# mLSTM and Fourier mixing on one core: recurrent outputs of batches 2 to 4 with tokens on partitions, and rows shifted by DMA

## The chip, the cores and the metric

The kernel runs on one core of a Trainium2 chip. The metric is the device time of one execution in microseconds (us). The time before is the median of three runs, 405.04 us (404.22, 408.13 and 405.04).

Five engines run their own instruction streams, each in order, and wait for each other by semaphores: TensorE (PE; its weight loads are shown apart as PEld), VectorE (DVE), ScalarE (ACT), GpSimd (POOL) and SyncE (SP). SP issues the DMAs of the kernel before. SBUF and PSUM have 128 partitions; a tile is written "partitions x elements".

## What is computed

Four batches, 8 heads, 768 tokens, 40 features per head, all float32. First a recurrence over tokens, per batch and head:

```python
for t in range(S):
    m_new  = np.maximum(f_gate[t] + m, i_gate[t])
    f_stab = np.exp(f_gate[t] + m - m_new); i_stab = np.exp(i_gate[t] - m_new)
    C = f_stab * C + i_stab * outer(v[t], k[t])      # 40 x 40
    n = f_stab * n + i_stab * k[t]                   # 40
    y[t] = sigmoid(o_gate[t]) * (C @ q[t]) / max(abs(n @ q[t]), 1)
```

Its output, with heads side by side, is x of 768 x 320 per batch. Then:

```python
u  = x + real(fft(fft(x, axis=seq), axis=feature))
un = (u - mean(u)) / sqrt(var(u) + 1e-6)
out = u + relu(un @ w1) @ w2                         # 320 -> 1280 -> 320
```

## The kernel before

**Order of the work.** A hand-written plan puts every piece of work at a place with `at(slot, phase, function, ...)`; pieces are sorted by slot and phase and issued in that order, which fixes the order on each engine. Within a slot the phases are EVAC, FILL, MAIN and FILL_PE. From slot 31 on, each batch's MLP owns the MAIN phase of 32 slots (batch 1: 31 to 62, batch 2: 63 to 94, batch 3: 95 to 126, batch 4: 127 to 158). What a later batch needs is filled in around it. For batches 2 to 4 (index b = 1 to 3) the first 20 slots are `mlp_block` (L1074), in rounds of four steps, in which TensorE writes bank after bank (pm), ScalarE copies the first product of a bank out and VectorE adds the others to the hidden layer (L1093); the next 12 slots are `mlp_out_pair` (L1191). Batch 1 uses an older form of both.

**The recurrence.** It runs in six chunks of 128 tokens. For batch 1 `plan_mlstm` plans it, with 128-token tiles. For batches 2 to 4 `plan_halves` does, with each chunk in two halves of 64 tokens, so that four products of 64 x 64 tiles run beside each other on TensorE (`product`, L491, tiles chosen by TILES). Chunk c starts at slot s = s0 + 3c; s0 is 32, 50 and 82 for batches 2, 3 and 4. In it:

- `halves_scores` and `halves_to_state` (TensorE): scores k by q into ps, and what the chunk adds to the state C; `halves_decay` (POOL, L629) and `halves_add` (VectorE, L638) update C;
- W is the table of decay weights: a DMA brings row maxima (M_d), ScalarE takes exponentials (L464), POOL masks it to causal (`mlstm_mask`, L487), VectorE multiplies it with the scores (`halves_weigh`, L643). `mlstm_scale_q` (POOL, L474) multiplies q with decays that a DMA brings from G_d;
- `halves_from_state` and `halves_from_chunk` (slot s+3): the output, numerator and the 41st column n @ q, into the head bank ph. Here the weights are C (or v) and the moving operand the queries (or W), 64 columns wide, so the output has features on partitions and tokens along the row. `halves_between` (L670) is a one-element ScalarE copy, warm, which separates the two halves of `halves_from_chunk`;
- `halves_gather` (ScalarE, L568 to L579) copies ph to SBUF as hT; `halves_turn` (TensorE, L681) transposes it in four pieces back into ph, tokens on partitions; `mlstm_finish` (VectorE, L696 to L703) makes the denominator and writes x, multiplied with the gate so.

The turns are at s0 + (7, 10, 13, 16, 19, 19) and the finishes one slot later. The last chunk has from-state and from-chunk in the MAIN phase, around an MLP matmul.

**Backward chunks.** The Fourier transform over tokens is folded: chunk pairs (0,5), (1,4) and (2,3) are added and subtracted (`mix_fold`, VectorE, L778 to L790). For this, chunks 2, 4 and 5 (BACKWARDS) are stored with their tokens reversed and shifted by one row. Before, that is done in `halves_gather`, which copies tokens reversed, with the odd token out handled by two small copies and by POOL (h_first). The folds of batches 3 and 4 are at s0 + 18 for the pair (2,3), s0 + 21 for (1,4) and s0 + 23 for (0,5). When x is folded, its tables are multiplied with the transform matrices (pz, pu), and its statistics follow.

**Set up on the way.** `halves_of_chunks` (L307 and on) makes the tables for batches 2 to 4 beside batch 1's recurrence: g to G_d (step 1), and with TensorE transposes and a spreading matmul colT and decB (steps 3 and 4). `maxima_out` writes M_d. colT holds per-token columns that ScalarE's exponentials and POOL's scaling of v (L480) use.

Of the kernel before, what the change touches and what calls it, by code (L numbers as in the profile page):

```python
# [10 lines left out]
FP = mybir.dt.float32  # L11
# [31 lines left out]
ORDER = (0, 5, 1, 4, 2, 3)  # L43
M_INIT = -1.0e30
# [8 lines left out]
def kernel(  # L53
# [87 lines left out]
    def gates(gp):  # L141
# [161 lines left out]

        def maxima_out():
            nc.sync.dma_start(out=M_d.rearrange("c i p t -> p c i t"), in_=M[0:BH].rearrange("p c (i t) -> p c i t", i=2))

        def halves_of_chunks(step):  # L307
# [8 lines left out]
            elif step == 1:  # L316
# [3 lines left out]
                nc.sync.dma_start(out=G_d[:, H:].rearrange("c p t -> p c t"), in_=g[H:BH])  # L320
# [12 lines left out]
            else:  # L333
                pt, pd = late["p2"]
                nc.vector.tensor_copy(out=colT[:, :, 1, H:], in_=pt[:, :, H:])  # L335
                nc.vector.tensor_copy(out=decB[:, NP:], in_=pd[:, NP:])

        at(12, FILL + 0.7, maxima_out)
        at(1, FILL + 0.2, parts, last)
# [9 lines left out]
        for n, (s, phase) in enumerate(((16, FILL + 0.2), (18, FILL + 0.3), (19, FILL + 0.4), (21, FILL_PE + 0.5),  # L349
                                        (26, FILL + 0.8))):  # L350
            at(s, phase, halves_of_chunks, n)
# [132 lines left out]
    def mlstm_mask(b, c):  # L484
        for i in range(2):
            W = chunks[b, c].W[i * LH:(i + 1) * LH]
            nc.gpsimd.affine_select(out=W, in_=W, compare_op=OP.is_ge, fill=0.0, base=0, pattern=[[0, H], [1, LH]],  # L487
                                    channel_multiplier=-1)
# [70 lines left out]
    def mlstm_heads(b, c, ph, parts=False):  # L559
# [3 lines left out]
        if b > 0:  # L563
            hT, before = (t.rearrange("p (hip m) t -> p hip m t", hip=2) for t in (hT, before))
        every, first, later = (tuple([slice(None)] * (len(ph.shape) - 1) + [t]) for t in
                               (slice(0, L), slice(0, 1), slice(1, L)))
# [27 lines left out]
    def side(n):  # L594
        return banks["heads"].rearrange("p hip (s m t) -> p s hip m t", s=2, t=L)[:, n]

    TILES = ((0, 0), (1, 1), (0, 1), (1, 0))

    def columns(c, n):

        return LH if c == 0 else n

    def halves_scores(b, c):
# [5 lines left out]
        for p in range(NP):  # L609
            for hip, i in TILES:  # L610
                r, t = slice(hip * 64, hip * 64 + D), slice(i * LH, (i + 1) * LH)
                product(k.ps[t, hip, p, :], k.qk[r, 1, p, t], k.qk[r, 0, p, t], True)

    def halves_to_state(b, c):
        k = chunks[b, c]
        for p in range(NP):
            for i, hip in TILES:
                if 2 * c + i < NS - 1:
                    r, h, n = slice(i * LH, (i + 1) * LH), hip * NP + p, columns(c, D)
                    product(k.pc[hip * 64:hip * 64 + n, i, p, :], k.k[r, h * D:h * D + n], k.vw[r, h, :], True)  # L620
# [11 lines left out]
    def halves_add(b, c, i):  # L632

        k, n = chunks[b, c], 2 * c + i
        if n == 0:
            nc.vector.tensor_copy(out=halves_state(k, 1), in_=k.pc[:, 0])
        elif n < NS - 1:
            nc.vector.tensor_tensor(out=halves_state(k, i + 1), in0=halves_state(k, i + 1), in1=k.pc[:, i], op=OP.add)  # L638
# [6 lines left out]
    def halves_from_state(b, c):  # L645

        k = chunks[b, c]
        k.ph = side(0)
        for m in range(2):
            for i in range(2):  # L650
                for hip, e in TILES:
                    if 2 * c + i > 0:
                        r, t, p = slice(hip * 64, hip * 64 + D), slice(i * LH, (i + 1) * LH), 2 * m + e
                        product(k.ph[e * 64:(e + 1) * 64, hip, m, t], k.C[i][r, p * D1:p * D1 + LH], k.qg[r, p, t],
                                m == 0 and i == (c == 0))

    def halves_from_chunk(b, c, turn):
# [4 lines left out]
        for m in range(2):  # L662
            for i, e in TILES:
                hip, n = i ^ turn, columns(c, D1)
                r, h = slice(i * LH, (i + 1) * LH), hip * NP + 2 * m + e
# [780 lines left out]
```

## Time and profile before

The profile is of one execution of 410.02 us, with a span of 408.3 us from first to last instruction, at a mean granted clock of 0.991 of full speed. That execution is 4.98 us over the median of the three timed runs.

| engine | busy us | share of span | instructions |
|---|---|---|---|
| TensorE matmul | 390.9 | 96% | 4246 |
| TensorE weight load | 285.3 | 70% | 4246 |
| VectorE | 281.3 | 69% | 669 |
| ScalarE | 182.1 | 45% | 510 |
| GpSimd | 129.1 | 32% | 228 |

| what the change touches | lines | time |
|---|---|---|
| transposes of the heads, 72 | PE L681 | 10.5 us, 275 ns each |
| ScalarE copies of the heads | L568, L575 | 583 and 588 ns each |
| finish, last product, 18 | DVE L703 | 8.8 us, 491 ns each |
| weighing of the scores, 18 | DVE L643 | 12.3 us, 682 ns each |
| DMA queue of all transfers | q1 | 35.8% of 16 engines' span |

How to read it: "busy" counts overlapping instructions of one engine once in the share and singly in a group's sum, so a group of matmuls that overlap has a sum that is longer than the time it takes. A row of a group names line, engine and operation, then output <- inputs, shapes and count, and after the bar busy time, mean time of one, and how long the engine had stood idle just before, with what ended it. In the list of waits, each row names an instruction, what it waited for, and the sum, the number and the longest of the waits. A slice line gives the busy share of 40 equal slices in tenths. "Issue" as a releaser means that the profile shows nothing the engine waited for.

### The profile page before, as it was taken

The page shows a single profiled execution, that of the slowest core. Times are in us where ns is not written, and L with a number is a line of the kernel's source. Part 1 is how long each engine was busy: PE and PEld are TensorE (multiplying, and loading weights), DVE is VectorE, ACT ScalarE, POOL GpSimd, SP SyncE. Part 2 cuts the span into 40 slices and gives each one's busy share as a digit, 9 for nine tenths or more (in the row PEclk, how much of TensorE's full clock was granted, in tenths as well). Part 3 has the DMA queues.
Part 4 walks back from the last instruction along what each step waited for, and adds up shares of the span by engine and source line. Part 5 has one row for each costly group of instructions (what it writes and reads, how often), then busy time and mean ns, then how long its engine had stood idle before and what let it go on. Part 6 is the DMA issues. An engine that isn't in the chain of part 4 may idle for free.

```text
span 408.3 us, 10669 instructions
## 1 busy us (share of the span) xinstructions
PE 390.9 (96%) x4246; PEld 285.3 (70%) x4246; DVE 281.3 (69%) x669; ACT 182.1 (45%) x510; POOL 129.1 (32%) x228
## 2 busy tenths in 40 slices
PE   8999999999979999998999999998999999999996
PEld 6877555556547677765559998855569997556996
DVE  8789986798846539675874579966764786335652
ACT  6987258577640232555464315553450122455000
POOL 5555314477940641240074233440230000020000
PEclk9999999989999999999999999999999999999999
DMA  7989499487643352375001444300000000000000
GB/s 217 289 229 309 114 232 270 157 240 216 166 119 109 113 136 86 99 206 161 0 10 36 139 122 151 108 4 2 0 2 6 28 33 34 0 0 2 32 34 32
DMA packets 23836, 43.29 MB, mean 106 GB/s; under 512 B 5076, under 2 KB 12972, under 8 KB 23660
## 3 DMA queue, kind: packets, MB, share of 16 engines
q1 hardware_dynamic: 23788, 42.63, 35.8%
q8 instruction: 33, 0.54, 0.6%
q14 instruction: 15, 0.12, 0.1%
HBM read 38.49 MB, written 4.12 MB: 104 GB/s over the span
## 4 chain that ended last, share of the span: by engine, by line
PE 80%; DVE 12%; issue 3%; ACT 3%; POOL 1%; POOLq 0%; DVEq 0%; ACTq 0%
PE po L1203 17%; PE pm L1084 16%; PE po L1147 8%; PE pm L1089 5%; PE pm L1022 5%; PE ph L491 4%; PE ps L491 3%; PE pu L901 3%; PE pz L870 2%; PE ph L681 2%; PE put L944 1%; DVE stats L928 1%; PE pm L1013 1%; PE pz L858 1%; PE ph L532 1%
## 5 line engine op out<-in xcount | busy, mean ns | idle before, releaser
L1153 DVE SCALAR_TENSOR_TENSOR x<-po,rstd,x 128x160 f32<-128x160 f32 (+1 forms) x69 | 26.9, 394 | 38.0 <-PE po L1203 35.3
L1093 DVE TENSOR_TENSOR h<-h,pm 128x384 f32<-128x384 f32 x60 | 30.7, 550 | 31.2 <-PE pm L1084 17.2
L1084 PE MATMUL pm<-uT,w_sb 128*128 128x384 f32 x90 | 37.3, 501 | 0.2 <-DVE uT L1072 0.2
L464 ACT ACTIVATE W<-W,colT 128x64 f32<-128x64 f32 x144 | 37.4, 340 | 0.0
L1147 PE MATMUL po<-w_sb,h 128*128 128x320 f32 x120 | 36.1, 451 | 0.0
L629 POOL TENSOR_TENSOR C<-C,decB 128x164 f32<-128x164 f32 x30 | 17.3, 577 | 55.8 <-DVE C L638 45.5
L487 POOL TENSOR_SCALAR_AFFINE_SELECT W<-W 64x512 f32<-64x512 f32 x36 | 28.3, 785 | 17.2 <-ACT W L464 16.1
L1022 PE MATMUL pm<-uT,w_sb 128*128 128x384 f32 x80 | 31.4, 521 | 0.6 <-issue 0.4
L1147 PEld LDWEIGHTS po<-w_sb,h 128*128 128x128 f32 x120 | 23.0, 196 | 10.0 <-issue 1.6
L1203 PE MATMUL po<-T,S 128*128 128x160 f32 x180 | 28.0, 302 | 0.2 <-DVE x L1153 0.2
L474 POOL TENSOR_TENSOR qg<-qk,Gb 128x512 f32<-128x512 f32 (+1 forms) x21 | 27.2, 1297 | 1.1 <-DMA Gb<-G_d 1.1
L1203 PEld LDWEIGHTS po<-T,S 128*128 128x128 f32 x180 | 25.4, 190 | 1.8 <-DVE x L1153 0.5
L1203 PE MATMUL po<-w_sb,h 128*128 128x160 f32 x180 | 26.4, 301 | 0.0
L1203 PEld LDWEIGHTS po<-w_sb,h 128*128 128x128 f32 x180 | 25.1, 190 | 1.2 <-DVE x L1153 0.3
L1089 PE MATMUL pm<-uT,w1t_sb 64*128 64x384 f32 x120 | 25.4, 510 | 0.0
L670 ACT COPY warm<-ph 1x1 f32<-1x1 f32 x18 | 2.6, 147 | 48.6 <-PE ph L491 44.9
L1084 PEld LDWEIGHTS pm<-uT,w_sb 128*128 128x128 f32 x90 | 15.5, 189 | 12.5 <-DVE h L1093 3.6
L1140 ACT ACTIVATE h<-h 128x384 f32<-128x384 f32 x45 | 23.1, 520 | 2.0 <-DVE h L1093 2.0
L968 POOL TENSOR_TENSOR t<-rstd 128x6 f32<-128x6 f32 x12 | 3.1, 256 | 65.3 <-DVE v L962 64.8
L949 ACT COPY uT<-put 128x384 f32<-128x384 f32 x24 | 11.1, 476 | 26.4 <-PE put L944 26.4
L480 POOL TENSOR_TENSOR vw<-kvt,colT 128x328 f32<-128x328 f32 x23 | 18.2, 792 | 13.6 <-DVE colT L335 11.0
L1022 PEld LDWEIGHTS pm<-uT,w_sb 128*128 128x128 f32 x80 | 14.7, 201 | 10.0 <-issue 3.4
(233 smaller groups left out, 879.8 us busy)
## 6 DMA issues: line engine op xcount, KB each, us to landing
kvt<-in_kv SPq DMA_DIRECT2D x24, 336.0 KB
qk<-in_qkT SPq DMA_DIRECT2D x48, 160.0 KB
raw<-in_w SPq DMA_DIRECT2D x10, 640.0 KB
Gb<-G_d SPq DMA_DIRECT2D x36, 128.0 KB
W<-M_d SPq DMA_DIRECT2D x36, 128.0 KB
so<-in_o SPq DMA_DIRECT2D x24, 160.0 KB
out<-x SPq DMA_DIRECT2D x24, 160.0 KB
ds_sb<-in_dft_s SPq DMA_DIRECT2D x1, 1155.0 KB
```

Source lines behind the costliest of these rows:

```text
L464: nc.scalar.activation(out=k.W[:, h, :], in_=M, func=AF.Exp, scale=-1.0, bias=colT[:, c, 0, b * H + h:b * H + h + 1])
L474: nc.gpsimd.tensor_tensor(out=k.qg[:, :, t], in0=k.qk[:, 0, :, t], in1=k.Gb[:, :, t], op=OP.mult)
L487: nc.gpsimd.affine_select(out=W, in_=W, compare_op=OP.is_ge, fill=0.0, base=0, pattern=[[0, H], [1, LH]], channel_multiplier=-1)
L491: nc.tensor.matmul(out, w, x, start=start, stop=True, skip_group_check=True)
L1022: nc.tensor.matmul(k.pm[i], w1_sb[:, ch, f0:f0 + L], u[2 * ch], start=(ch == 0 and not ahead), stop=(ch == 1 and ahead), skip_group_check= ...
L1084: nc.tensor.matmul(bank, w, u, start=start, stop=True, skip_group_check=True)
L1089: nc.tensor.matmul(bank, block(w1t_sb, i)[rows], mlp_u(gr, 1)[rows], start=False, stop=True, skip_group_check=True)
L1093: nc.vector.tensor_tensor(out=h, in0=h, in1=bank, op=OP.add)
L1140: nc.scalar.activation(out=h, in_=h, func=AF.Relu, scale=-1.0)
L1147: nc.tensor.matmul(k.po, hidden(gr, f)[:, i * L:(i + 1) * L], w2_sb[:, f, :], start=(f == 0), stop=(f == NFF - 1))
L1153: nc.vector.scalar_tensor_tensor(out=u, in0=po, scalar=k.rstd[:, c:c + 1], in1=u, op0=OP.mult, op1=OP.add)
L1203: nc.tensor.matmul(po, a[:, f], w[:, f], start=start and f == 0, stop=f == half - 1, skip_group_check=True)
```

## The change

Batches 2 to 4 get their recurrent outputs with tokens on partitions. In `halves_from_state` and `halves_from_chunk` weights and moving operand change places: the weights are the queries (or W), the moving operand is C (or v), 41 columns. The output is in the form that the finish reads, so `halves_gather` and `halves_turn` are gone, and the finish comes one slot after the products (s + 4), with the tanh of the gate at s + 3. The last chunk is planned as the others are.

Reversal of the chunks 2, 4 and 5 moves to the inputs: queries and gate are reversed on the host, the mask runs with a step of −1, and the tables M_d and G_d are written reversed (POOL copies, and DMAs in pieces). The shift by one row stays: for these chunks the finish writes its product into so, and `halves_rows`, at s + 5, moves rows 0 to 126 of it to rows 1 to 127 of x, and row 127 to a row 0, by two DMAs that ScalarE issues. For chunk 2 POOL also copies two single rows.

The two halves of odd head pairs are exchanged in v, k and the columns (`token_major` on the host, `other_halves` and the copies to colT in the kernel); `halves_add` reads the banks in turn. Step 3 of `halves_of_chunks` moves from slot 21 to 24, and s0 of batches 3 and 4 from 50 and 82 to 53 and 85; the folds, planned from s0, move with it.

```diff
+        def other_halves():
+            odd = [colT[i * LH:(i + 1) * LH, :, 0, H + 1:BH:2] for i in range(2)]
+            kept = gp.tile([LH, NT, (BH - H) // 2], FP, name="kept")
+            for out, in_ in ((kept, odd[0]), (odd[0], odd[1]), (odd[1], kept)):
+                nc.gpsimd.tensor_copy(out=out, in_=in_)
         def maxima_out():
-            nc.sync.dma_start(out=M_d.rearrange("c i p t -> p c i t"), in_=M[0:BH].rearrange("p c (i t) -> p c i t", i=2))
+            m, in_ = (t.rearrange("p (n t) -> p n t", t=LH) for t in (free[0:BH, 0:S], flat(M, slice(0, NT))))
+            for c0, c1, back in RUNS:
+                n = slice(2 * c0, 2 * c1)
+                nc.gpsimd.tensor_copy(out=m[:, n], in_=backwards(in_[:, n], LH - 1, LH) if back else in_[:, n])
+            m = m.rearrange("p (c i) t -> p c i t", i=2)
+            for odd in range(2):
+                for i in range(2):
+                    nc.sync.dma_start(out=M_d[:, i ^ odd, odd:BH:2].rearrange("c p t -> p c t"), in_=m[odd:BH:2, :, i])
...
-                nc.sync.dma_start(out=G_d[:, H:].rearrange("c p t -> p c t"), in_=g[H:BH])
+                turned = x_bufs[1].rearrange("p c m -> p (c m)")[0:BH, 2 * S:2 * S + 3 * L].rearrange("p (c t) -> p c t", t=L)
+                at_ = 0
+                for c0, c1, back in RUNS:
+                    v = g[0:BH, c0:c1]
+                    if back:
+                        v = turned[:, at_:at_ + c1 - c0]
+                        at_ += c1 - c0
+                        nc.gpsimd.tensor_copy(out=v, in_=backwards(g[0:BH, c0:c1], L - 1, L))
+                    nc.sync.dma_start(out=G_d[c0:c1, H:].rearrange("c p t -> p c t"), in_=v[H:BH])
...
-                nc.vector.tensor_copy(out=colT[:, :, 1, H:], in_=pt[:, :, H:])
+                nc.vector.tensor_copy(out=colT[:, :, 1, H:BH:2], in_=pt[:, :, H:BH:2])
+                for i in range(2):
+                    nc.vector.tensor_copy(out=colT[i * LH:(i + 1) * LH, :, 1, H + 1:BH:2],
+                                          in_=pt[(1 - i) * LH:(2 - i) * LH, :, H + 1:BH:2])
...
+        at(13, FILL + 0.7, other_halves)
...
-        for n, (s, phase) in enumerate(((16, FILL + 0.2), (18, FILL + 0.3), (19, FILL + 0.4), (21, FILL_PE + 0.5),
+        for n, (s, phase) in enumerate(((16, FILL + 0.2), (18, FILL + 0.3), (19, FILL + 0.4), (24, FILL_PE + 5.4),
...
+        base, step = (LH - 1, -1) if c in BACKWARDS else (0, 1)
         for i in range(2):
             W = chunks[b, c].W[i * LH:(i + 1) * LH]
-            nc.gpsimd.affine_select(out=W, in_=W, compare_op=OP.is_ge, fill=0.0, base=0, pattern=[[0, H], [1, LH]],
+            nc.gpsimd.affine_select(out=W, in_=W, compare_op=OP.is_ge, fill=0.0, base=base, pattern=[[0, H], [step, LH]],
...
+    def queries(c, i):
+        return rows(1 - i if c in BACKWARDS else i)
...
+            for hip, j in TILES:
+                r, i = slice(hip * 64, hip * 64 + D), j ^ (p & 1)
+                product(k.ps[rows(j), hip, p, :], k.qk[r, 1, p, rows(i)], k.qk[r, 0, p, queries(c, i)], True)
...
+        v, state = k.pc[:, i], halves_state(k, i + 1).rearrange("p (m two) d -> p m two d", two=2)
+        step, bank = D1, k.pc[:, 1].offset - k.pc[:, 0].offset
+        new = bass.AP(tensor=v.tensor, offset=v.offset,
+                      ap=[list(v.ap[0]), [2 * step, NP // 2], [step + (-bank if i else bank), 2], [1, D1]])
         if n == 0:
-            nc.vector.tensor_copy(out=halves_state(k, 1), in_=k.pc[:, 0])
-        elif n < NS - 1:
-            nc.vector.tensor_tensor(out=halves_state(k, i + 1), in0=halves_state(k, i + 1), in1=k.pc[:, i], op=OP.add)
+            nc.vector.tensor_copy(out=state, in_=new)
+        else:
+            nc.vector.tensor_tensor(out=state, in0=state, in1=new, op=OP.add)
...
-        k.ph = side(0)
+        k.ph = banks["heads"][:, :, 0:NP * D1].rearrange("p hip (m d) -> p hip m d", d=D1)
+        for p in range(NP):
+            for hip, i in TILES:
+                if 2 * c + i > 0:
+                    r = slice(hip * 64, hip * 64 + D)
+                    t = queries(c, i)
+                    product(k.ph[t, hip, p, :], k.qg[r, p, t], k.C[i][r, p * D1:(p + 1) * D1], p == 0)
+    def halves_from_chunk(b, c, turn):
+        k = chunks[b, c]
         for m in range(2):
-            for i in range(2):
-                for hip, e in TILES:
-                    if 2 * c + i > 0:
-                        r, t, p = slice(hip * 64, hip * 64 + D), slice(i * LH, (i + 1) * LH), 2 * m + e
-                        product(k.ph[e * 64:(e + 1) * 64, hip, m, t], k.C[i][r, p * D1:p * D1 + LH], k.qg[r, p, t],
-                                m == 0 and i == (c == 0))
-    def halves_from_chunk(b, c, turn):
-        k = chunks[b, c]
-        for m in range(2):
-            for i, e in TILES:
-                hip, n = i ^ turn, columns(c, D1)
-                r, h = slice(i * LH, (i + 1) * LH), hip * NP + 2 * m + e
-                product(k.ph[e * 64:e * 64 + n, hip, m, r], k.v[r, h * D1:h * D1 + n], k.W[r, h, :], False)
+            for j, i in TILES:
+                p, hip = 2 * m + (i ^ j), j ^ turn
+                h = hip * NP + p
+                product(k.ph[queries(c, i), hip, p, :], k.W[rows(j), h, :], k.v[rows(j), h * D1:(h + 1) * D1],
+                        2 * c + i == 0 and m == turn == 0)
...
-    def halves_gather(b, c):
-        k = chunks[b, c]
-        k.hT = hT_bufs[(b * NT + c) % 2]
-        mlstm_heads(b, c, k.ph)
-    def halves_turn(b, c):
-        k = chunks[b, c]
-        px = side(0 if c == NT - 1 else 1)
-        for p in range(NP):
-            nc.tensor.transpose(px[:, p // 2, p % 2], k.hT[:, p, :], ident)
-        k.px = px
...
+        h1 = k.px.rearrange("p (a pr) (two e) -> p a (pr two) e", a=2, two=2) if b == 0 else k.ph
...
+        k.x = k.so if b > 0 and c in BACKWARDS else xs[b][:, c, 0:DM]
+        x, sc = (t.rearrange("p (a h d) -> p a h d", a=2, d=D) for t in (k.x, k.so))
         nc.vector.tensor_tensor(out=x, in0=h1[:, :, :, 0:D], in1=sc, op=OP.mult)
+    def halves_rows(b, c):
+        x, y = xs[b][:, :, 0:DM], chunks[b, c].x
+        def move(out, in_):
+            nc.scalar.dma_start(out=out, in_=in_)
+        if c == 2:
+            nc.gpsimd.tensor_copy(out=x[0:1, 2], in_=x[0:1, 0])
+            nc.gpsimd.tensor_copy(out=x[0:1, 0], in_=x[0:1, 1])
+        if c in BACKWARDS:
+            move(x[1:L, c], y[0:L - 1])
+            move(x[0:1, 1 if c == 2 else c], y[L - 1:L])
...
-            at(s + 3, MAIN - 0.1 if end else FILL_PE, halves_from_state, b, c)
-            at(s + 3, MAIN - 0.1 if end else FILL_PE, halves_from_chunk, b, c, 0)
-            at(s + 3, MAIN if end else FILL_PE + 0.5, halves_between, b, c)
+            at(s + 3, FILL_PE, halves_from_state, b, c)
+            at(s + 3, FILL_PE, halves_from_chunk, b, c, 0)
+            at(s + 3, FILL_PE + 0.5, halves_between, b, c)
             at(s + 3, FILL_PE + 3, halves_from_chunk, b, c, 1)
-            at(s + 4, FILL - 0.6, halves_gather, b, c)
-            at(s + 4, FILL + 0.35, mlstm_tanh, b, c)
-            t = s0 + (7, 10, 13, 16, 19, 19)[c]
-            at(t, FILL_PE + 0.5, halves_turn, b, c)
-            at(t + 1, MAIN + 0.55, mlstm_finish, b, c)
+            at(s + 3, FILL + 0.35, mlstm_tanh, b, c)
+            at(s + 4, FILL + 0.3 if b == 1 else MAIN + 0.55, mlstm_finish, b, c)
+            at(s + 5, MAIN + 0.2, halves_rows, b, c)
...
-    plan_batch(2, 50, 83, s_mlp + 2 * MLP_SLOTS)
-    plan_batch(3, 82, 115, s_mlp + 3 * MLP_SLOTS)
+    plan_batch(2, 53, 83, s_mlp + 2 * MLP_SLOTS)
+    plan_batch(3, 85, 115, s_mlp + 3 * MLP_SLOTS)
...
+        t = t.reshape(B, H, NT, L, D).transpose(0, 2, 3, 1, 4).copy()
+        t[1:, :, :, 1::2] = np.roll(t[1:, :, :, 1::2], LH, axis=2)
+        return t
+    qs = feature_major(q)
+    qs[1:, list(BACKWARDS)] = qs[1:, list(BACKWARDS), ..., ::-1]
+    qkT = np.stack([qs, feature_major(k)], axis=4)
     v1 = np.concatenate([token_major(v), np.ones((B, NT, L, H, 1), v.dtype)], axis=-1)
     kv = np.concatenate([v1.reshape(B, NT, L, H * D1), token_major(k).reshape(B, NT, L, H * D),
                          np.zeros((B, NT, L, LH - D), k.dtype)], axis=-1)
-    o = o_gate.transpose(0, 2, 1, 3).reshape(B, S, DM)[:, _tokens()]
+    o = o_gate.transpose(0, 2, 1, 3).reshape(B, NT, L, DM).copy()
+    o[0] = o[0].reshape(S, DM)[_tokens()]
+    o[1:, list(BACKWARDS)] = o[1:, list(BACKWARDS), ::-1]
```

## The prediction

> **What bounds the kernel now.** I read the page's busy shares by slice first, then its chain.
>
> ```profile
> PE   8999999999979999998999999998999999999996
> DVE  8789986798846539675874579966764786335652
> ...
> PE 80%; DVE 12%; issue 3%; ACT 3%; POOL 1%; POOLq 0%; DVEq 0%; ACTq 0%
> ```
>
> TensorE is nine tenths busy nearly everywhere and has 80% of the chain, so an instruction taken from it counts in full, unless VectorE (12%) then becomes late. VectorE is close behind early on: between 72 and 112 us it works 34.6 of 40 us. Next, the groups by shape, for what one instruction costs:
>
> ```profile
> L491 PE MATMUL ph<-W,kvt 64*41 64x64 f32 x480 | 13.0, 217 | 1.3 <-ACT warm L670 0.7 <-DVE W L643 0.5
> L491 PE MATMUL ph<-qg,C 40*64 40x64 f32 x528 | 11.9, 225 | 4.5 <-DVE x L703 4.3 <-POOL W L487 0.2
> L681 PE MATMUL ph<-ident,h 128*128 128x128 f32 x72 | 10.5, 275 | 0.0
> L703 DVE TENSOR_TENSOR x<-ph,so 128x320 f32<-128x320 f32 x18 | 8.8, 491 | 0.6
> ```
>
> The 72 transposes and the two products of the outputs are what the change touches; the means (275 ns) overlap, so durations are taken from the timeline. Last, TensorE's waits:
>
> ```profile
> PE ph L491 <- DVE x L703: 4.3, 6, 1.3
> PE ps L491 <- issue: 2.1, 1, 2.1
> ...
> PE ph L491 <- ACT warm L670: 0.7, 1, 0.7
> PE ph L491 <- DVE W L643: 0.5, 1, 0.5
> ```
>
> 4.3 us are a chunk's first product waiting until the output of an earlier chunk has been read from the one head bank.
>
> The profiled run took 410.02 us, 4.98 over the median of 405.04. I explain that by the stall called "issue": 2.1 us at 117 us without a releaser, after which the granted clock is 0.51 for 3.5 us (120.6 to 124.1), some 1.7 us lost. It needn't recur, so I add my sum to the median.
>
> **The change, part by part** (us, minus is faster).
>
> 1. *Transposes gone.* In the timeline four begin at 86.99 and TensorE's next matmul at 87.43: 0.44 a chunk, on a full engine. 18 chunks: −7.9.
>
> 2. *Tokens become the weights' columns; the moving operand shrinks from 64 columns to 41.* No row has these forms. Four concurrent tiles take 61 ns (32 matmuls of from-state in 0.48 us) and 50 to 58 in from-chunk; the nearest row, 64-column weights with a 41-column moving operand (to-state of chunk 0), takes 52, and the narrowest, 40 by 41, 38. So nothing to −0.17 a chunk (0 to −3.0); with the nearest row −0.09: −1.6.
>
> 3. *The decay spread's transposes and matmul* (0.87 us at 47.95) move to slot 24, where batch 1's recurrence leaves gaps. Between 0 and −0.75: −0.5.
>
> 4. *The head bank comes free three slots earlier.* −4.3 by the wait above. But chunk 5's from-state now follows chunk 4's finish (0.16 + 0.17 + 0.20 + 0.49 + 0.49 = 1.5 us of VectorE) and chunk 5's weighing (0.68) more closely; 0 to 1.5 in batches 3 and 4, I take 1.0 each: +2.0.
>
> 5. *The last chunk's second half of from-chunk* loses the matmuls that lay between it and the ScalarE copy it waits for. The same wait was 0.75 at 82 us. 0 to 0.75 for three batches, 0.45 taken: +1.35.
>
> 6. *Batch 2's finish* stands at FILL+0.3, ahead of chunk 1's weighing and copy, whose waits are the 0.5 and 0.7 above. 1.5 us of VectorE and a tanh (0.48) get in front; 0 to +3, taken +2.0.
>
> 7. *Off the path, at nothing:* four POOL copies and three more SP issues for M_d, two and three for G_d (SP's issues take 0.35; the tables behind them are used over 1 us later), three POOL copies of colT, 0.35 of VectorE. They lie beside batch 1's recurrence; without that cover some 1 us. ScalarE loses its copies of the heads (about 0.75 a chunk) and gets 18 DMA issues (0.35 to 0.6 by SP's row); it is 45% busy. What queues behind a row move on ScalarE (the MLP's bank copies and relus) waits for that chunk's finish, which by then is done.
>
> Sum so far −7.9 − 1.6 − 0.5 − 4.3 + 2.0 + 1.35 + 2.0 = **−8.9**.
>
> 8. *The row moves.* Nine chunks go to x by a DMA of 127 rows of 1280 B, SBUF to SBUF; before has none. The nearest row is the output's store, 128 rows of the same size:
>
> ```profile
> DMA  0000000000004699997996310000000000000000
> ...
> DMA packets 144, 0.16 MB, mean 82 GB/s; under 512 B 16, under 2 KB 144, under 8 KB 144
> ```
>
> That is 2 us from 329.5 on, in slices of 0.05: 128 row packets and 16 small ones (one per engine) in 0.60 us, each row 55 ns (tenth to ninetieth percentile of all such rows: 54 to 72), the first 0.84 after the issue. On 16 engines a move lands in 1.45 us; on one, in 0.84 + 127 × 0.055 = 7.9 us. Which? The 3,157 four-byte packets in the whole trace, which end each transfer once per engine, are within one of what the transfers give if each uses the largest number of engines, up to 16, that divides its partitions (16 for 128, 10 for 40, 12 for 24). 127 is prime, so I take one. The Trainium skill ("DMA: Bandwidth & Descriptors", "Why a DMA increments its semaphore by 16 and not by 1") says just this: the largest divisor up to 16, and one engine for 127 partitions. By it the move costs what the next paragraph works out; without it 1.45 us, hidden.
>
> VectorE's fold waits for the moves, and VectorE is in order. In batches 3 and 4 this happens beside the MLP block, whose four steps take 0.65, 1.3, 2.8 and 1.3 us on TensorE. Count from the end of the step-1 slot in which chunk 5's recurrence starts. Chunk 4's finish ends at 2.8 + 0.4 + 0.6 + 1.5 = 5.3; its move runs 6.2 to 13.2. Chunk 5's is issued by about 10 and, on the same engine, runs 13.2 to 20.3. VectorE asks for chunk 4 (fold 1,4) at 10.9 and waits 2.4; that fold (1.8), a sum of w2 (0.98), the statistics (0.6) and an MLP add (0.55) end at 17.2; it asks for chunk 5 (fold 0,5) and waits to 20.3, folds to 22.1, adds at 22.6. TensorE's tail matmuls, ready at 15.1, need the first add (17.2, wait 2.1), and after 1.1 more the next block needs a bank freed by the second (18.3 to 22.6, wait 4.3). Without the moves the same counting leaves 0.9. So +5.5 a batch, **+11.0** for two. In batch 2 chunk 5's move is issued near 120.5 and the fold comes at 133.06: 4 us to spare, nothing.
>
> 9. *Clock.* In before, stalls of 2.3 us (117) and of 0.7 and 0.9 close together (80, 82) were followed by a granted clock of 0.5 for 3.5 us; two of 1.4 (186, 275) were not. Part 8's are longer. 0 to 1.7 a batch; as VectorE is catching up then, I take +0.9 in all. The Trainium skill ("TensorE: Matmul & The Clock Gate", "Part 1: The HAM clock gate") has half clock follow an idle window of 3.4 us that runs free. By it the price is 0 or 1.7 with the luck of the window; in before far less idleness sufficed.
>
> Sum: −8.9 + 11.0 + 0.9 = +3.0, **408.0 us**, 0.7% above the median. By the bounds alone: with every gain whole and moves hidden 389; with 72 ns a row and no small gain about 418.
>
> **The rivals.**
>
> *A, the forecast:* the moves take one engine and eat the gain. Its own range is 403 to 411 (a stall of 3.5 to 7 a batch). For: the packet count and the counting of part 8. Against: the fold's place in VectorE's queue is reckoned from other slots' durations. Chance 0.50.
>
> *B, the moves are hidden:* they spread over 16 engines, or the folds come later than reckoned. 405.0 − 8.9 = 396.1. For: DMA is idle at 196 to 212 in before, and the shown stores of the same size land in 1.45. Against: no transfer of before has a prime number of partitions. Chance 0.28.
>
> *C, slower:* the rows within SBUF take longer than the store's. At 72 ns a move runs 9.1, chunk 5's lands 4.2 later, and TensorE pays that again in each batch: 408.0 + 8.4 = 416. It decides from 0.55 us a pair of moves on (4 ns a row), where the time passes 409.1. For: the fold waits for the second move with nothing behind to cover it; against: the isolated stores keep 55. Chance 0.22; in it also lies that VectorE, saturated between 72 and 112 us, gives batch 2's transposes (6 × 0.44) nothing.
>
> **How the numbers follow.** Faster or slower by over 1% (4.05 us) is about what a measurement here can tell from no change. A: 0.1 faster, 0.6 within, 0.3 slower. B: 0.96 faster. C: all slower. Faster 0.05 + 0.27 = 0.32; within 0.30 + 0.01 = 0.31; slower 0.15 + 0.22 = 0.37. The range, 394 to 414, takes in B with 2 us either way, all of A and a third of C.
>
> **What would show it.** No transposes on ph, 72 matmuls and as many weight loads fewer; TensorE's wait for the finish gone from its list. Row moves at about 8 us to landing (A) or 1.5 (B); the subtract-and-add folds of batches 3 and 4 with DMA as releaser, 2 and 3 us; TensorE waiting for the MLP add (L1093's line) 5 to 6 us a batch near both folds. I am wrong if the moves land early, if TensorE stalls elsewhere (from-chunk on the copy, over 3 us), or if VectorE's gaps near the folds hide the wait.

## The result, and the profile after

The changed kernel takes 446.1 us (median; 441.35 to 446.97), the kernel before beside it 406.59. The ratio is 1.0946, with a 95% interval of 1.0834 to 1.1058: 8 to 11% slower, far outside the forecast range of 394 to 414.

The profiled execution took 446.84 us, with a span of 445.1 and a mean granted clock of 0.939 (before: 0.991). First the page of the kernel after: busy tenths by slice, the granted clock, and the chain.

```profile
PE   8998999797999999598979998869869999999997
DVE  8799885976544585435655678734555478444562
ACT  6977365654222225333323233525324012345100
PEclk9999999796989999869989999969878999999999
...
PE 51%; DMA 7%; DVE 7%; ACT 3%; ACTq 2%; issue 1%; POOL 1%; SPq 1%; DVEq 0%
```

TensorE has holes that were not there before, and in the same slices and the ones after them the granted clock falls. TensorE's share of the chain is 51% where it was 80%; DMA (7%) and ScalarE's own queue (ACTq, 2%) are new in it. No engine has become the bound: VectorE is at 62% and ScalarE at 39%, both lower than before. What got longer is waiting. TensorE's list of waits, after (sum, times, longest):

```profile
PE ph L519 <- ACT warm L702: 10.0, 7, 3.1
PE pm L1121 <- ACT h L1157: 8.9, 2, 5.4
PE pm L1116 <- DVE h L1125: 7.9, 2, 4.1
PE po L1235 <- DVE x L1185: 3.0, 3, 1.4
PE ph L519 <- DVE W L675: 1.3, 1, 1.3
```

The 4.3 us on the finish, which the change was to remove, are down to 0.8, but 19 us on ScalarE (the small copy warm, and the MLP's bank copy h) and 8 on VectorE (the MLP add h) have come. All of TensorE's waits from 60 us on add up to 33 us after and 9 before, 24 more. The rest is the clock. In the traces the granted clock is either 1 or 0.5, so time at half clock is 2 × (1 − 0.939) × 445 = 54 us after and 2 × (1 − 0.991) × 408 = 7 us before; on a full engine each such microsecond loses half of itself, so 47 more cost up to 23. With the work saved, 24 + 23 − 8 = 39; the two profiled spans lie 36.8 apart. The pages' busy times say the same: TensorE stands idle 24.2 us longer than before (445.1 − 403.5 against 408.3 − 390.9), and is busy 12.6 us longer although the transposes are gone.

The products themselves, after, by shape:

```profile
L519 PE MATMUL ph<-kvt,W 64*64 64x41 f32 x576 | 17.5, 241 | 11.3 <-ACT warm L702 10.0 <-DVE W L675 1.3
L519 PE MATMUL ph<-C,qg 40*64 40x41 f32 x528 | 13.0, 239 | 0.8 <-DVE so L723 0.8
```

The transposes are gone, and 41 columns move instead of 64; what stands before the products is the wait on warm.

**How ScalarE holds TensorE.** ScalarE's timeline after (start, duration, engine, line; in brackets the idle time before and its end):

```profile
180.51 0.48 ACT L1148 COPY h<-pm 128x384 f32<-128x384 f32 x1 [0.49 <-PE pm L1116]
182.16 5.44 ACTq L731 DMA_DIRECT2D x<-so  x2
187.64 1.06 ACT L491 ACTIVATE W<-W,colT 128x64 f32<-128x64 f32 x4 [6.65 <-DMA qk<-in_qkT]
188.61 0.45 ACT L608 ACTIVATE so<-so 128x320 f32<-128x320 f32 x1
188.97 0.46 ACT L1157 COPY h<-pm 128x384 f32<-128x384 f32 x1
```

and TensorE's in the same stretch:

```profile
183.13 0.92 PE L1121 MATMUL pm<-uT,w1t_sb 64*128 64x384 f32 x4 [0.34 <-DVE h L1125]
189.48 1.64 PE L1121 MATMUL pm<-uT,w1t_sb 64*128 64x384 f32 x2 [5.43 <-ACT h L1157]
```

The two issues of chunk 2's move in batch 3 keep ScalarE for 5.44 us: the first takes 0.66, the second, a single row, 4.67. (The profile names the load of qk as what ended the idle time; the row of the issue above it shows where it went.) Behind them stand the exponentials, the tanh and the bank copy L1157 that TensorE needs. At 102 us, with batch 2's chunk 2, it is another wait, on GpSimd. ScalarE first, then GpSimd:

```profile
99.84 0.73 ACT L414 ACTIVATE m<-m 128x640 f32<-128x640 uint32 x1
103.38 0.57 ACTq L731 DMA_DIRECT2D x<-so  x1
104.00 1.06 ACT L491 ACTIVATE W<-W,colT 128x64 f32<-128x64 f32 x4 [3.43 <-POOL C L655]
```

```profile
99.72 0.20 POOL L1000 TENSOR_TENSOR t<-rstd 128x6 f32<-128x6 f32 x1 [2.16 <-DVE v L994]
...
102.40 0.44 POOL L734 COPY x<-x 1x320 f32<-1x320 f32 x1
102.90 0.45 POOL L735 COPY x<-x 1x320 f32<-1x320 f32 x1
```

Chunk 2's single row may not land before GpSimd has copied away what it overwrites (L734, L735); those copies queue behind the normalization's steps, and these behind VectorE. Three engines in order, and TensorE stood 3.1 us at the end of it.

ScalarE also waits for the finish itself. VectorE's last product of chunk 4 in batch 3, then ScalarE:

```profile
206.28 0.49 DVE L723 TENSOR_TENSOR so<-ph,so 128x320 f32<-128x320 f32 x1
```

```profile
205.93 0.49 ACT L1168 ACTIVATE h<-pm 128x384 f32<-128x384 f32 x1 [0.17 <-PE pm L1116]
206.85 1.23 ACTq L731 DMA_DIRECT2D x<-so  x2
```

ScalarE is done at 206.42, the product at 206.77, and the issue starts at 206.85. In four of the nine moves ScalarE stands 0.4 to 0.7 us in this way before it can issue.

**How the move itself holds TensorE.** The DMA view of 206.5 to 223.5 us, in which only chunk 4's and chunk 5's moves of batch 3 are under way (slices of 0.43 us):

```profile
GB/s 0 0 0 6 12 59 12 12 24 24 24 27 24 24 24 24 27 24 24 24 27 12 18 15 6 24 24 27 24 24 24 27 24 24 24 24 27 24 12 0
...
q10 hardware_dynamic: 320, 0.33, 5.9%
```

A steady 24 GB/s is one row of 1280 B per 54 ns, one after the other, and 5.9% is about one engine in sixteen. Issued at 206.85, chunk 4's rows have left by 215.5; chunk 5's, issued at 214.29, follow them, and the last leaves at 222.9: 14.8 us for 254 rows. VectorE, then TensorE:

```profile
219.39 0.56 DVE L1125 TENSOR_TENSOR h<-h,pm 128x384 f32<-128x384 f32 x1
223.60 0.49 DVE L810 TENSOR_TENSOR eo<-x 128x320 f32<-128x320 f32 x1 [3.66 <-DMA x<-so]
```

```profile
220.50 1.56 PE L1121 MATMUL pm<-uT,w1t_sb 64*128 64x384 f32 x8
225.80 0.91 PE L1116 MATMUL pm<-uT,w_sb 128*128 128x384 f32 x2 [3.74 <-DVE h L1125]
```

The fold waits 3.66 us for the move, the adds behind it come as much later, and TensorE waits 3.74.

### The profile page after: what moved, and what is told of

It reads as the page before. It is cut to its first block, busy times and chain, and to the rows that moved or that the text cites. A ratio compares the mean times of both kernels' runs of the same rounds, so it can differ in the third digit from the quotient of the medians.

```text
span 445.1 us, 10555 instructions
## 1 busy us (share of the span) xinstructions
PE 403.5 (91%) x4174; PEld 288.9 (65%) x4174; DVE 276.6 (62%) x671; ACT 171.4 (39%) x480; POOL 131.8 (30%) x237
## 4 chain that ended last, share of the span: by engine, by line
PE 51%; DMA 7%; DVE 7%; ACT 3%; ACTq 2%; issue 1%; POOL 1%; SPq 1%; DVEq 0%
PE po L1235 17%; PE pm L1116 14%; DMA x<-so 7%; PE po L1179 5%; PE pm L1121 3%; PE ph L519 3%; ACTq L731 2%; PE ps L519 2%; PE pu L933 2%; PE pz L890 1%; ACT W L491 1%; PE put L976 1%; DVE h L1125 1%; DVE x L1185 1%; PE pzt L890 1%
## 5 line engine op out<-in xcount | busy, mean ns | idle before, releaser
L1116 PE MATMUL pm<-uT,w_sb 128*128 128x384 f32 x90 | 42.6, 568 | 8.1 <-DVE h L1125 7.9
L515 POOL TENSOR_SCALAR_AFFINE_SELECT W<-W 64x512 f32<-64x512 f32 x36 | 25.3, 703 | 34.2 <-ACT W L491 32.9
L1121 PE MATMUL pm<-uT,w1t_sb 64*128 64x384 f32 x120 | 27.0, 524 | 9.2 <-ACT h L1157 8.9
L1054 PE MATMUL pm<-uT,w_sb 128*128 128x384 f32 x80 | 33.7, 565 | 0.1
L1116 PEld LDWEIGHTS pm<-uT,w_sb 128*128 128x128 f32 x90 | 17.8, 213 | 24.5 <-DVE h L1125 14.0
L1179 PEld LDWEIGHTS po<-w_sb,h 128*128 128x128 f32 x120 | 23.2, 197 | 10.3 <-issue 1.9
L501 POOL TENSOR_TENSOR qg<-qk,Gb 128x512 f32<-128x512 f32 (+1 forms) x21 | 28.4, 1354 | 0.1
L519 PE MATMUL ph<-kvt,W 64*64 64x41 f32 x576 | 17.5, 241 | 11.3 <-ACT warm L702 10.0
L1121 PEld LDWEIGHTS pm<-uT,w1t_sb 64*128 64x128 f32 x120 | 12.7, 189 | 21.8 <-ACT h L1157 10.1
L1054 PEld LDWEIGHTS pm<-uT,w_sb 128*128 128x128 f32 x80 | 16.3, 217 | 12.0 <-issue 5.3
```

The costliest lines, as they stand in the source:

```text
L501: nc.gpsimd.tensor_tensor(out=k.qg[:, :, t], in0=k.qk[:, 0, :, t], in1=k.Gb[:, :, t], op=OP.mult)
L519: nc.tensor.matmul(out, w, x, start=start, stop=True, skip_group_check=True)
L1054: nc.tensor.matmul(k.pm[i], w1_sb[:, ch, f0:f0 + L], u[2 * ch], start=(ch == 0 and not ahead), stop=(ch == 1 and ahead), skip_group_check= ...
L1116: nc.tensor.matmul(bank, w, u, start=start, stop=True, skip_group_check=True)
L1121: nc.tensor.matmul(bank, block(w1t_sb, i)[rows], mlp_u(gr, 1)[rows], start=False, stop=True, skip_group_check=True)
L1179: nc.tensor.matmul(k.po, hidden(gr, f)[:, i * L:(i + 1) * L], w2_sb[:, f, :], start=(f == 0), stop=(f == NFF - 1))
```

## The experiments

Three theories: "one engine" (the move is slow and the folds wait), "issue" (ScalarE is held), "plan" (finish, last chunk, slots).

### The moves: who issues them, and in how many pieces

**e1, issued by SyncE.**

```diff
         def move(out, in_):
-            nc.scalar.dma_start(out=out, in_=in_)
+            nc.sync.dma_start(out=out, in_=in_)
```

> The row moves are issued by SyncE in place of ScalarE; nothing else changes. In the changed kernel's trace ScalarE's DMA issues take 3.2 to 4.7 us in five of nine pairs, and TensorE then waits for ScalarE (5.6 us at 184, 3.6 at 290, 3.2 at 102, 1.8 at 122). Theory 'issue' (ScalarE is held while it issues a move): these four stalls of 14 us and the half clock behind them go, about 420 us; the two stalls at the folds (3.9 and 4.3 us) stay. Theory 'one engine' (the loss is the folds' wait for a transfer on one DMA engine): 440 to 447, no gain. Theory 'plan' (finish, last chunk, slots): 440 to 447 as well.

Measured: 433.12 us, ratio 1.0656 (1.0609 to 1.0704). 13 us less, between what the theories had; the bank copy's 8.9 us are gone from TensorE's waits. But the folds cost more than in the changed kernel, because the work in front of them comes earlier by more than the rows do. For batch 2's chunk 5 VectorE now waits from 127.7 to 135.8 us, in the changed kernel from 136.0 to 138.3. TensorE's waits:

```profile
PE pm L1116 <- DVE h L1125: 9.7, 2, 4.9
...
PE pz L902 <- DVE fe L817: 6.0, 1, 6.0
```

The second row is batch 2's fold, for which the prediction had 4 us to spare. ScalarE is not wholly free either, because loads share the one engine with the move. Of a load of so issued at 103.11, behind a move, fifteen sixteenths have landed by 105.53 and the last only at 110.34, just behind the move's 127 rows (109.84) and single row (110.04); ScalarE's tanh waits 1.2 us for it, and TensorE then 1.3 on warm.

**e2, the 127 rows as 112 and 15.**

```diff
-            move(x[1:L, c], y[0:L - 1])
+            move(x[1:113, c], y[0:112])
+            move(x[113:L, c], y[112:L - 1])
```

> Each move of 127 rows is made of two, 112 rows and 15 rows, still issued by ScalarE. 112 is a multiple of 16. Theory 'one engine': each lands in 1.5 to 2 us, the folds' waits of 10 us on VectorE and TensorE's stalls of 3.9 and 4.3 us go. If ScalarE is held because one DMA engine's queue is full of the 127 rows, the 3 to 5 us holds go too, and the time is within some 3 us of the kernel without moves. If it is held because SyncE's loads are being issued at the same time, the holds stay or grow with a third issue, and the time is 425 to 435. Theory 'plan': above 435.

Measured: 423.28 us, ratio 1.0413 (1.0363 to 1.0464). The 127 rows of one move now go within 1.13 us where nothing else moves (from 208.36 on, say), against 14.8 for the two above. The time is far from the kernel without moves all the same (e3). No fold waits for a DMA any more, and no issue is held (0.52 to 0.85 each, one of 1.41). What is left is ScalarE, for which three issues are 2.0 us, beside the waits for the finish and, in batch 2, for GpSimd (3.0 us on TensorE again). Its timeline in this run, and TensorE's:

```profile
199.12 2.01 ACTq L731 DMA_DIRECT2D x<-so  x3
201.18 0.47 ACT L608 ACTIVATE so<-so 128x320 f32<-128x320 f32 x1 [2.48 <-DMA x<-so]
201.55 0.51 ACT L1173 ACTIVATE h<-h 128x384 f32<-128x384 f32 x1
201.97 0.13 ACT L702 COPY warm<-ph 1x1 f32<-1x1 f32 x1
```

```profile
199.70 0.44 PE L519 MATMUL ph<-kvt,W 64*64 64x41 f32 x16
202.15 0.44 PE L519 MATMUL ph<-kvt,W 64*64 64x41 f32 x16 [2.01 <-ACT warm L702]
```

**e3, no moves.** The rows of chunks 2, 4 and 5 stay unshifted.

```diff
-        k.x = k.so if b > 0 and c in BACKWARDS else xs[b][:, c, 0:DM]
+        k.x = xs[b][:, c, 0:DM]
...
-        if c in BACKWARDS:
-            move(x[1:L, c], y[0:L - 1])
-            move(x[0:1, 1 if c == 2 else c], y[L - 1:L])
```

> The row moves are left out: the finish writes its product straight to x, unshifted, so x has its rows of chunks 2, 4 and 5 in the wrong place; the order of all other work is the changed kernel's. Theories 'issue' and 'one engine' together: stalls of 22 us and most of 48 us at half clock go, 403 to 412 us, and what is left over the forecast without moves (396) is the plan's. Theory 'plan': above 430.

Measured: 402.61 us, ratio 0.9917 (0.9883 to 0.9951). So the moves cost 43.5 us, and everything else in the change gains 3.2 against the 405.84 beside it. This run also measures the clock's share, since its matmuls are the changed kernel's. Of the 44.3 us between the two profiled spans (445.1 and 400.8), TensorE was idle for 23.4 more and busy for 20.9 more (403.5 against 382.6) with the same 4174 matmuls: that is what the lower clock cost (51 us more at half clock, 25 at most).

**e5, both cures:** e1 and e2 in one kernel.

> Both cures together: the moves are split into 112, 15 and 1 rows and issued by SyncE. The theory so far has the moves' price of 43.5 us (446.1 against 402.6 without them) in three mechanisms, all of which multiply by the half clock: one DMA engine per move, ScalarE held, ScalarE's own issue time. Then nothing is left but the wait of SyncE itself: 403 to 408 us, with no stall of TensorE on ScalarE's bank copies and none at the folds. If instead SyncE, which now waits for each finish, brings the later loads too late: 412 to 425, with waits for loads.

Measured: 403.06 us, ratio 0.99 (0.9835 to 0.9964). The moves are as good as free, and this version is faster than both kernels, by about 1% than the one before (the interval is 0.4 to 1.7%). No fold waits for a DMA, and TensorE's wait on warm is what it is without moves:

```profile
PE ph L519 <- ACT warm L702: 3.4, 6, 1.1
```

The four cases:

| issued by | 127 rows in one | 112 + 15 rows |
|---|---|---|
| ScalarE | 446.1 | 423.3 |
| SyncE | 433.1 | 403.1 |

The one engine costs 30 us when SyncE issues and 23 when ScalarE does; issuing by ScalarE costs 20 with short moves and 13 with long ones. They overlap by 7; that a stall of the one covers part of the other is the likely reason. Time at half clock in these four, by the same rule from clock and span: 54, 27, 31 and 7 us.

**e6, ScalarE busy without a DMA.** No moves; in their place four copies of a dead tile.

```diff
+        if c in BACKWARDS:
+            for _ in range(4):
+                nc.scalar.copy(out=chunks[b, c].so, in_=chunks[b, c].so)
```

> No moves (as in the run without them, x unshifted); in their place ScalarE copies a dead tile of 128 x 320 onto itself four times, 4 x 0.46 = 1.8 us, about as long as the three issues of the split moves (0.55, 0.85 and 0.56). This has no DMA and no wait for GpSimd. Theory 'ScalarE's issue time is the price that the split left' : stalls of 2 us at the copy between the halves of from-chunk and at the bank copies come back, with half clock, 410 to 418 us. If the split's remaining 20.7 us came from DMAs: 402 to 405.

Measured: 418.32 us, ratio 1.03 (1.0219 to 1.0382), 15.7 more than without them. TensorE's waits in this run:

```profile
PE ph L519 <- ACT warm L702: 7.7, 7, 1.8
...
PE pm L1121 <- ACT h L1157: 2.6, 2, 1.5
```

These are the rows of the changed kernel, without any DMA. The four copies took 1.93 us each time. Like the issues, they also wait for the finish, 0.4 to 0.9 us in five of the nine places; how the price divides between the two was not measured. Nine times some 2 us on an engine that is 39% busy in the changed kernel cost 15.7 us: it is the place in ScalarE's queue that costs. Of the 15.1 us between the two profiled spans TensorE was idle for 8.0 more and busy for 7.1 more. In e3 the first row is 3.4 and the second absent.

**e12, the single row first.**

```diff
-            move(x[1:L, c], y[0:L - 1])
             move(x[0:1, 1 if c == 2 else c], y[L - 1:L])
+            move(x[1:L, c], y[0:L - 1])
```

> The changed kernel with the two DMAs of a move in the other order: the single row is issued first, then the 127 rows; both still by ScalarE. In the changed kernel the second issue, the single row behind 127 rows on one DMA engine, is the one that takes 1.4 to 4.7 us in six of nine moves, while the first takes 0.63 to 0.66 in eight. If the hold comes from issuing behind an unfinished 127-row transfer: both issues take 0.55 to 0.7, except chunk 5's first, which follows chunk 4's transfer; TensorE's stalls on ScalarE's bank copies (5.6 and 3.6) shrink to 1.5 to 2 as with the split, the folds' waits stay, 430 to 438 us. If the hold belongs to the time or to SyncE's loads: the second issue takes 3 to 5 us again, 442 to 448.

Measured: 443.03 us, ratio 1.0881 (1.0808 to 1.0953). The time is where the other reading had it, the issues are where the first had them. The rows of the issues (ns: least, median, most), after and in e12:

```profile
L731 ACTq DMA_DIRECT2D x<-so x18: 552/654/4665, 98.4 to 320.2; - x18
```

```profile
L731 ACTq DMA_DIRECT2D x<-so x18: 537/628/1154, 102.9 to 317.1; - x18
```

The hold is gone, and even chunk 5's first issue, with chunk 4's rows still moving, took 0.54, against the expectation. So it is not an unfinished transfer that holds ScalarE; the long issues came only straight behind the one for 127 rows. The time barely fell because TensorE's wait at the folds grew (10.1 us on the add in two stalls, 7.3 at batch 2's fold in one), as in e1, and because batch 2's chunk 2 now waits for GpSimd ahead of both issues: TensorE's longest wait on warm is 4.3 us, 3.1 in the changed kernel.

### The plan

**e4, the kernel before with the later slots only.**

```diff
-    plan_batch(2, 50, 83, s_mlp + 2 * MLP_SLOTS)
-    plan_batch(3, 82, 115, s_mlp + 3 * MLP_SLOTS)
+    plan_batch(2, 53, 83, s_mlp + 2 * MLP_SLOTS)
+    plan_batch(3, 85, 115, s_mlp + 3 * MLP_SLOTS)
```

> The kernel before with the recurrences of batches 3 and 4 three slots later (53 and 85), nothing else of the change. If the later slots cost or bring nothing by themselves: 403 to 407 us. If they push the folds into the MLP block's add steps and stall TensorE there: 409 to 415. A gain (under 401) would say that the prediction left a term out.

Measured: 412.4 us, ratio 1.0145 (1.0094 to 1.0195). In that kernel two finishes, a fold, a sum of w2 and statistics then stand together in VectorE's queue, and TensorE waits for the add behind them; this is 3.0 of the 6.6 us:

```profile
PE pm L1089 <- DVE h L1093: 3.0, 2, 1.9
```

In e5, with the same slots and the early finish, this row is absent.

**e7, e5 with slots 50 and 82.** Batches 1 and 3 share one buffer for x. The early finish then writes batch 3's x over rows of batch 1's x that the last outputs have yet to read, so this kernel changes part of the computation; the later slots are a condition of the early finish.

```diff
-    plan_batch(2, 53, 83, s_mlp + 2 * MLP_SLOTS)
-    plan_batch(3, 85, 115, s_mlp + 3 * MLP_SLOTS)
+    plan_batch(2, 50, 83, s_mlp + 2 * MLP_SLOTS)
+    plan_batch(3, 82, 115, s_mlp + 3 * MLP_SLOTS)
```

> As the split moves on SyncE, with the recurrences of batches 3 and 4 at 50 and 82 again. In the kernel before, three slots later alone cost 6.6 us. If that holds here too: 5 to 7 us less than with 53 and 85. If the later slots were needed for the early finish (VectorE's 1.5 us in other slots; the two stalls of 1.5 us at 240 and 252 on the output's sum stay or move): equal or slower by up to 8.

Measured: 404.21 us, ratio 0.996 (0.9923 to 0.9996): no gain. What the slots cost in e4 they don't cost here.

**e8, e5 with batch 2's finish at MAIN+0.55.**

```diff
-            at(s + 4, FILL + 0.3 if b == 1 else MAIN + 0.55, mlstm_finish, b, c)
+            at(s + 4, MAIN + 0.55, mlstm_finish, b, c)
```

> As the split moves on SyncE, with batch 2's finish at MAIN+0.55, as batches 3 and 4 have it. The prediction charged the early place with 2.0 us (weighing and copy of chunk 1 behind 1.5 us of VectorE). If right: the stalls of 1.5 and 1.3 at 81 to 84 shrink to 0.7 and 0.9, the half clock behind them stays or goes, 1 to 3 us less. If the finish is then late for chunk 2's from-state: equal or slower.

Measured: 403.84 us, ratio 0.9908 (0.9873 to 0.9944), the same as e5. The two waits at 81 to 85 us go and no half clock is left in the span (1.0), but from-state then waits at 81, 97 and 106 us, 1.4, 0.9 and 2.0 us.

**e9, e5 with the first two finishes of batch 4 one slot later.**

```diff
-            at(s + 4, FILL + 0.3 if b == 1 else MAIN + 0.55, mlstm_finish, b, c)
-            at(s + 5, MAIN + 0.2, halves_rows, b, c)
+            if b == 3 and c < 2:
+                at(s + 5, MAIN + 0.65, mlstm_finish, b, c)
+            else:
+                at(s + 4, FILL + 0.3 if b == 1 else MAIN + 0.55, mlstm_finish, b, c)
+            at(s + 6 if b == 3 and c < 2 else s + 5, MAIN + 0.2, halves_rows, b, c)
```

> Split moves on SyncE, and the finish of chunks 0 and 1 of batch 4 one slot later (s + 5, MAIN + 0.65). TensorE's two stalls of 1.5 us at 241 and 253 wait for VectorE's output sum (x of the residual, line of po), which stands behind that finish of 1.5 us. If that finish is the cause: both stalls go, 2 to 3 us less than 403.1. If VectorE is simply full in these slots: the stalls move, no change (402 to 404).

Measured: 404.27 us, ratio 0.9934 (0.9901 to 0.9966). The output sum no longer waits, from-state does; e5's row, then e9's:

```profile
PE po L1236 <- DVE x L1186: 3.0, 3, 1.4
```

```profile
PE ph L519 <- DVE x L723: 3.3, 2, 2.5
```

**e10, e5 with the last chunk planned as before.**

```diff
-            at(s + 3, FILL_PE, halves_from_state, b, c)
-            at(s + 3, FILL_PE, halves_from_chunk, b, c, 0)
-            at(s + 3, FILL_PE + 0.5, halves_between, b, c)
+            end = c == NT - 1
+            at(s + 3, MAIN - 0.1 if end else FILL_PE, halves_from_state, b, c)
+            at(s + 3, MAIN - 0.1 if end else FILL_PE, halves_from_chunk, b, c, 0)
+            at(s + 3, MAIN if end else FILL_PE + 0.5, halves_between, b, c)
```

> Split moves on SyncE, and the last chunk planned as before: its two first products ahead of the MLP's matmuls in MAIN, the copy behind them. This undoes the prediction's part 5 (charged with 1.35 us for three batches). If right: the stalls of 0.5 us at 116, 190 and 279 go, about 1.5 us less than 403.1; if the earlier place makes from-state wait longer for chunk 4's finish or chunk 5's weighing: no change or up to 2 us more.

Measured: 404.29 us, ratio 0.996 (0.9928 to 0.9993), no gain: the wait on warm falls from 3.4 to 2.4, and that on the finish (so L723) rises from 0.8 to 2.1.

**e11, e9 and e10 together.**

> Both of these changes in one kernel. If they add: 398 to 400.5 us, faster than the kernel before by 1.5 to 2%. If one of them only moves its stall: 401 to 403.

Measured: 406.27 us, ratio 1.0009 (0.9983 to 1.0035), above both expectations: they don't add, and the gain of e5 is lost. In its trace from-state's stall of 2.5 us at 243 is followed by 3.4 us at half clock; the same stall in e9 is not.

## Why the prediction was wrong

**The step that failed most is part 7.** It put ScalarE's 18 issues "off the path, at nothing", because ScalarE is 45% busy and loses its copies of the heads. It did not ask what waits for the time that issuing takes: issuing by ScalarE in place of SyncE costs 13 us with long moves and 20 with short ones, and plain copies of 1.93 us in the issues' place cost 15.7 (e6). It also took the finish, for which what queues behind a move waits, to be done by then; in four of nine moves ScalarE stood 0.4 to 0.7 us for it. Two more things lengthened the hold: the second issue behind the 127 rows (up to 4.67 us), and chunk 2's wait for GpSimd. By the plan ScalarE's copies were removed at other places in its queue, so their 0.75 a chunk was no credit here.

In the sum, the moves were forecast at 11.0 + 0.9 = 11.9 us and cost 43.5. Of the 31.6 missing, 13 are ScalarE's part with the long moves; 18 more are the one engine's (30 against 11.9, parts 8 and 9). With the short moves as the starting point it is 20 and 11.

**Part 9, the clock, was mis-sized:** +0.9 was taken, 3.4 at most. The changed kernel spends 54 us at half clock, in nine stretches of 3.4 to 10.2 us, and this cost 20.9 us against e3, about as much as the added idle time. The forecast let only the folds' stalls trigger it; in fact stalls at ScalarE were followed by it too. As a single term of the sum it is off by the most, but it comes with the stalls, and so it is part of the 31.6 above, not more. (The prediction's 0.7 and 0.9 for the stalls at 80 and 82 us are 0.5 and 0.7 in the rows that it shows.)

**Part 8 was right in mechanism, and near in size for the two folds it reckoned.** The 127 rows run on one DMA engine: 7.4 us a move in the pair shown, 8.2 to 9.6 for chunk 2's moves, which run beside SyncE's loads, against 7.0 reckoned; and 8.6 from issue to the last row for chunk 5 of batch 3 against 10.3. TensorE's stalls at the folds are 3.7 and 4.1 us, against 5.5 a batch; with those at ScalarE shortened they are 4.8 and 4.9 (e1), 4.7 and 5.4 (e12), so that the stalls at ScalarE had delayed the folds already. Batch 2's "4 us to spare, nothing" was wrong in e1 and e12, where its fold cost TensorE 6.0 and 7.3. In the changed kernel chunk 5's move there was issued at 125.7, not near 120.5, and its rows ran behind chunk 4's until 137.0, not 128; as the fold came late as well, TensorE waited only 0.2. The forecast priced this whole mechanism at 11.0 + 0.9; e1 against e5 says 30, stalls and clock together.

**Parts 1 to 6 were −8.9 and came out as −3.2** (e3, interval −4.7 to −2.0).
- Part 1 holds: TensorE's time from the start of a transpose to the next instruction sums to 8.0 us before, and is nothing after.
- Part 2 was mis-sized: −1.6 was taken by the nearest row. From the first of from-state's 32 matmuls to the next instruction it is 0.49 to 0.52 us before and 0.49 to 0.51 after, and from-chunk's 16 take 0.23 at best in both, so 41 columns in place of 64 bring −0.5 at most.
- Part 4's 4.3 us went down to 0.8. What is left is chunk 5's from-state behind chunk 4's finish, 0.4 in batches 3 and 4, where 1.0 each was put; in e10, with from-state earlier, it is 1.0 each.
- Parts 5 and 6 were sized about right as stalls: 3.4 on warm where 0.7 was, and 1.3 on the weighing where 0.5 was, 3.5 more against the 3.35 put. But undoing either (e10, e8) gains nothing: VectorE's 1.5 us of finish have to stand somewhere between two products and the next weighing, and TensorE waits on one side or the other.
- Not foreseen: the output sum of batch 2's MLP waits behind batch 4's finish, 3.0 us (before: 0.2); e9 moves it to another place, at the same size.
- Part 3 was not measured by itself. The parts as measured come to −8.0 − 0.5 − 3.5 + 3.5 + 2.8 = −5.7, so 2.5 us have no account of their own. The clock may take them: e3's executions were granted 0.991 to 0.996, which on 401 us is worth 1.6 to 3.6, while two thirds of the executions of before beside them had 1.0.

**The rivals.** B's premise, that the moves are spread over 16 engines, is what e5 makes true, and its time, 396.1, was missed by 7 us for the reasons just given. C had the right side but the wrong cause: the median row packet of each move took 55 to 60 ns, and the pair above 58 a row; what was not reckoned is the engine that issued them, and the clock.

What stays open: how ScalarE's part divides between the issues themselves and their waits for the finish, and why a second issue straight behind a 127-row one is held for 0.55 in some cases and 4.67 in others. The longest three (3.4 to 4.7) fell into stretches with SyncE's loads under way, but 1.4, 1.8 and 3.2 also came with none.

## What to carry to other kernels

Before a DMA issue is put on a computing engine, look at what stands behind it in that engine's queue, and price the issue, and its wait for what it moves, like an instruction there; here an engine's share of busy time (39%) said nothing of it. Choose row counts that divide: 112 + 15 rows in place of 127 turned 7.4 us into 1.1. And when TensorE is full, reckon each stall of a microsecond or two with the half clock that may follow it: here the clock cost about as much (20.9 us) as the stalls themselves (23.4).

## What was not expected of the hardware

- Stalls of 1.3 and 1.1 us within 4 us (e5, at 81 to 85) came with 6.8 us at half clock from 83.7 on, and in e6 four stalls of 1.5 to 1.8 each came with 3.4 to 6.8. The length of a stall does not decide it by itself: the same two stalls at 81 to 86 came with 3.4 us in e3 and with none in e6, and 2.0 us alone (e8, at 108) with none. Before a kernel's end the stretches are 3.4, 6.8 or 10.2 us long. What else decides is not shown here.
- The Trainium skill ("TensorE: Matmul & The Clock Gate", "Part 1: The HAM clock gate") puts the ramp penalty under 1% of a typical kernel span, where it speaks of a kernel's first matmuls. Here 54 of 445 us in the middle of a kernel ran at half clock and cost 20.9 us, 5%.
- A DMA issue directly behind the one for 127 rows took up to 4.67 us on ScalarE and 3.25 on SyncE; in the other order, or behind a split move, 0.5 to 0.9 with one or two of 1.1 to 1.4.
- The pace of four concurrent small tiles went with the weights, not with what moves: from-state takes 61 ns for four at best (32 matmuls in 0.49 us) with 64 columns moving and with 41, from-chunk 56 to 58 (16 in 0.23). With 41 columns moving in both, to-state takes 52 with 64 weight columns and 38 with 40.
